# Another order of the units of one pair of heads, and the last product's polynomial regrouped in place in PSUM

## The chip, the cores and the metric

The kernel runs on one core of one Trainium2 chip. The metric is the device time of one execution in microseconds (us). It is taken as the median of several runs, and one further run was recorded by the profiler. The engines are named as the profile names them: PE (TensorE; PEld is its weight load), DVE (VectorE), ACT (ScalarE), POOL (GpSimd) and SP (SyncE, which in this kernel issues every DMA; SPq is its queue).

## What is computed

The reference runs three parts, each on the output of the one before it.

```python
# 1. attention by hash buckets: q, k, v are (2, 8, 768, 64), proj is (64, 6)
mask = q_bucket[:, :, :, None] == k_bucket[:, :, None, :]     # 6 sign bits of q @ proj and k @ proj
scores = np.where(mask, scale * np.matmul(q, k.transpose(0, 1, 3, 2)), -1000000000.0)
attn = softmax(scores)                                        # along the last axis
attn_out = np.matmul(attn, v)                                 # -> x of shape (1536, 512)
# 2. soft mixture of 8 experts with 4 slots each
logits = x @ phi                                              # (1536, 32)
slot_input = softmax(logits, axis=0).T @ x
slot_out[e] = np.maximum(slot_input[e] @ w1[e], 0.0) @ w2[e]
x = softmax(logits, axis=1) @ slot_out
# 3. the last product
h = x @ w_in                                                  # w_in is (512, 2048)
g = h - np.tanh(h)
out = g @ w_out                                               # w_out is (2048, 512)
```

## The kernel before, in words

**Attention** works on eight pairs of heads. Everything that is done for a pair is cut into units, and the strings `START`, `STEP` and `LAST` (lines 64 to 71) write out by hand in which order the units are issued. `STEP` is gone through once for each of the pairs 0 to 6, `LAST` for pair 7 (loop at line 709). Every engine executes what it is given in program order, so the string is the order of each engine's queue, SP's too. The map `role` (line 660) says for which pair a unit works: while the scores of pair i are made, units such as `m`, `l0` to `l3`, `d` and `f2` prepare pair i + 1, `t0`, `t1`, `b`, `h0` to `h3` and `kc` prepare pair i + 2, `qk` loads pair i + 3, and `xr`, `xe` and others that begin with x, and `lg`, finish pair i - 1. The units that matter here:

- `s0`, `s1` (`s_unit`, lines 493 to 513): one tile of 128 x 768 scores of one head, four matmuls into a PSUM tile (L497, L499). ACT takes the exponential (L501), POOL adds it to a running sum (L506, L512).
- `m` (`m_unit`, L446 and L447): two matmuls into a PSUM tile and a row maximum on DVE. There are twelve in a pair.
- `a` (`av_unit`, L520 and L524): the product with v, eight matmuls into PSUM tiles of its own. It does nothing while its two exponentials have not been issued.
- `l0` to `l3` (`lo`, L429, L431, L433, L436): the low halves of k and q, one subtraction of 64 x 768 on DVE each, with both inputs in SBUF. `l2` (L433) reads the copy that `kc` makes, `l3` (L436) one that `d` makes.
- `kc` (`kh1_copy`, one DMA kh<-KA) and `d` (`dups`, two or four DMAs QB<-QA and KB<-KA): copies from SBUF to SBUF.
- `wl` and `wc` (`win_load`, `win_cvt`): one 512 KB load of a piece of w_in into one of two buffers, and its conversion: ACT L174 and three DVE instructions (L178, L187, L192) by way of a PSUM tile `cl`. A `wl` issues nothing while two pieces wait for conversion.
- `t0`, `t1` (transposes, L353), `b` (`bits`, L362, after which eight DMAs QA<-rt and KA<-rt write the rows that `m` and `s` of that pair need), `f2` (`m_fin`, five or six DMAs QA<-row and z<-zrow), `v` (one load), `v1` (`v_unit`, three additions on POOL, L474 to L476), `v2`, `h0` to `h3` (ACT L406), `xr`, `xe`, `x2`, `x3` (L535 to L584), `lg` (`logits`, L594), `qk` (`load_qk`, four DMAs tq and tk, L321), `lp` (one 1 MB piece of the experts' weights, from pair 5 on), and `e00` to `e03` (work of pair 5 alone).

All PSUM tiles of these units but those of `a` come from one pool of three buffers (`ps`, line 272). A unit's first matmul therefore waits until an earlier unit's reader has freed a buffer.

**The experts** (`moe`, with the order `MOE`) follow. They read 32 pieces of 1 MB, and eight more of w_out, each through a ring of SBUF slots that open as attention closes its pools.

**The last product** (`class Ffn`) goes in 32 steps n, 16 blocks of h for each of two halves of the tokens. A step's block of h is 128 x 768 in two PSUM tiles `ph` of 512 and 256 columns. `h_mm` (L1167) makes them, `h_sq` has ACT write z = h^2 and w = (z + Q_A)^2 to SBUF (L1174, L1175), and `h_g` has DVE make g = Q_C h z (w + Q_B), a polynomial that stands for h - tanh(h). `split_hi` (ACT, L1205) and `split_lo` (POOL, L1210) split g into two parts, and `mm` multiplies them by w_out: six times three matmuls of 512 columns in a step (L1229 to L1231). In the steps of the first half, DVE also converts one block of w_out in each step (`cv_a2`, `b1`, `b2`: L178, L187, L192, all from SBUF to SBUF), and ACT and POOL split it (L1123, L1124). The first blocks are issued by the orders `MOE` and `RUN`, the rest by the loop at line 1254.

Of the kernel before, what the change touches and what calls it, by code (L numbers as in the profile page):

```python
# [15 lines left out]
ALU = mybir.AluOpType  # L16
# [33 lines left out]
Q_C = 17.0 / 315.0  # L50
Q_A = -(2.0 / 15.0) / (2.0 * Q_C)
Q_B = (1.0 / 3.0) / Q_C - Q_A * Q_A
# [12 lines left out]
        "h3.0 wq1p.0 m.0 m.0 m.0 l0.0 m.0 const.2 m.0 v.0 wk1a.0 m.0 m.0 m.0 wq0p.0 m.0 kc.0 m.0 "  # L65
        "m.0 qk.1 l2.0 m.0 wl.0 d.0 wc.0 wk0s.0 t0.1 f2.0 h1.1 t1.1 l1.0 h3.1 l3.0 v1.0 h2.1 "
        "kc.1 oi.1 b.1 v2.0 wc.0 wc.0 h0.1 qk.2 oi.2 wl.0").split()
STEP = ("s0 l1 d s1 a lp m xe s0 m xr e00 v m s1 m s0 l0 m lp m a m s1 l2 v1 m a m m m l3 a wl lp "
        "wc t1 s0 t0 s1 s0 m e01 h0 lp a lp h1 x2 lp wl f2 e02 s1 h3 lp v2 b e03 x3 wc wl s0 s1 "
        "h2 kc a lp wl wc lg qk").split()  # L70
LAST = ("s0 lp lp a s0 xe lp s1 s0 xr lp a s1 x2 x3 lg a lp s1 s0 s0 s0 lp s1 a s1 a s1 lp a lp").split()


# [52 lines left out]
def body(ctx: ExitStack, tc: tile.TileContext, q, k, v, proj, phi, w1, w2, w_in, w_out, cst, out, dbg=None):  # L126
    nc = tc.nc
# [7 lines left out]
    lg = const.tile([P, B * KT, NS], F32, name="lg")  # L135
# [114 lines left out]
    def attention():  # L250
# [458 lines left out]
        for i in range(NPR):  # L709
            for u in STEP if i < NPR - 1 else LAST:  # L710
                n = i + role.get(u, role.get(u[0], 0))
# [414 lines left out]
    class Ffn:  # L1126
# [49 lines left out]

        def h_g(self, n, p):
            z, w, g = self.views(n, p)
            nc.vector.scalar_tensor_tensor(w, w, Q_B, z, ALU.add, ALU.mult)  # L1179
            nc.vector.scalar_tensor_tensor(g, w, Q_C, self.ph[p], ALU.mult, ALU.mult)  # L1180


        def h_any(self, n):
# [155 lines left out]
```

## Time and profile before

| what | us |
|---|---|
| median of 3 runs | 519.05 (517.33 to 519.7) |
| the profiled execution, its own time | 519.88 |
| span of the profiled execution, first to last instruction | 518.0 |
| busy in that span: PE / PEld | 474.7 / 302.3 |
| busy in that span: DVE / ACT / POOL | 352.2 / 272.1 / 294.3 |

The time of the profiled execution is 1.9 us longer than its span: what lies around the program's first and last instruction. Its own time is 0.83 us above the median of the runs. All starts in the rows are us from the start of the span. A busy PE isn't PE at its peak, since matmuls are pipelined and a matmul's row includes its latency. PEclk is the share of TensorE's full clock that was granted.

### The profile page before, as it was taken

Reading aid. Unit: us, or ns where it says so; the run is one execution under the profiler, and the core shown is the slowest. Engines: PE = TensorE matmul, PEld = TensorE weight load, DVE = VectorE, ACT = ScalarE, POOL = GpSimd, SP = SyncE. Lnnn points to the kernel's source line nnn. Section 1 sums busy time; section 2 is a strip of 40 time slices with the busy share of each in tenths; the row PEclk is TensorE's granted clock in tenths of the full one; section 3 lists DMA queues with packets and bytes.
Section 4 is the critical chain, followed back from the end, with each engine's and each line's share of the span. In section 5 each row is a group of like instructions: output and inputs, shape, how many; then the busy total and the mean of one; then the engine's idle time right before and its main releaser. Section 6 shows DMA issues by size and latency. Waiting matters only on the chain.

```text
span 518.0 us, 7441 instructions
## 1 busy us (share of the span) xinstructions
PE 474.7 (92%) x2634; PEld 302.3 (58%) x2634; DVE 352.2 (68%) x493; ACT 272.1 (53%) x463; POOL 294.3 (57%) x243
## 2 busy tenths in 40 slices
PE   8798888998989989999999899889888888999996
PEld 3444555555545556565565634447666666888884
DVE  4949478696696776837622664569999998655552
ACT  6253654736537446364334111167777766767662
POOL 3867766777677677786874120025665664544442
PEclk9659899999999999999999999998999999999999
DMA  6518146091451712937679699994000000200003
GB/s 206 121 29 233 42 105 199 13 249 42 119 142 49 195 62 51 329 134 226 213 266 376 253 369 388 356 407 192 1 1 0 2 0 34 88 1 1 1 1 127
DMA packets 51572, 72.83 MB, mean 141 GB/s; under 512 B 25604, under 2 KB 33480, under 8 KB 51528
## 3 DMA queue, kind: packets, MB, share of 16 engines
q1 hardware_dynamic: 51528, 72.28, 42.9%
q8 instruction: 23, 0.38, 0.3%
q14 instruction: 21, 0.17, 0.1%
HBM read 60.08 MB, written 3.15 MB: 122 GB/s over the span
## 4 chain that ended last, share of the span: by engine, by line
PE 58%; DVE 32%; DMA 3%; SPq 3%; issue 2%; ACT 1%; DVEq 0%; ACTq 0%
PE pav L524 9%; DVE mx L447 9%; PE pst L497 6%; PE po L1229 5%; PE po L1230 5%; PE po L1231 5%; PE pst L499 5%; DVE win L1179 4%; PE pm L446 4%; DVE win L192 3%; DVE KB L429 3%; DVE win L1180 3%; DVE win L178 2%; DMA w<-in_moe_w_dram 2%; PE pl L594 2%
## 5 line engine op out<-in xcount | busy, mean ns | idle before, releaser
L512 POOL TENSOR_TENSOR es<-es,e 128x768 f32<-128x768 f32 x59 | 115.9, 1976 | 32.6 <-ACT e L501 32.2
L501 ACT ACTIVATE e<-pst 128x768 f32<-128x768 f32 x96 | 76.1, 809 | 87.7 <-PE pst L499 83.6
L447 DVE TENSOR_REDUCE mx<-pm 128x1 f32<-128x768 f32 x96 | 87.6, 953 | 36.8 <-PE pm L446 35.0
L524 PE MATMUL pav<-e,tv 128*64 128x256 f32 (+1 forms) x384 | 74.5, 506 | 0.0
L1210 POOL TENSOR_TENSOR split<-win,split 128x512 fp32r<-128x512 f32 x31 | 39.9, 1286 | 53.9 <-ACT split L1205 53.6
L1179 DVE SCALAR_TENSOR_TENSOR win<-win 128x512 f32<-128x512 f32 x64 | 51.0, 797 | 26.9 <-ACT win L1175 26.9
L497 PE MATMUL pst<-QA,KA 128*128 128x512 f32 x192 | 56.7, 377 | 10.8 <-DVE win L192 4.5
L446 PE MATMUL pm<-KA,QA 96*128 96x512 f32 x192 | 53.1, 380 | 2.6 <-DVE mx L447 1.1
L1210 POOL TENSOR_TENSOR ghl<-win,ghl 128x256 fp32r<-128x256 f32 x32 | 27.5, 859 | 47.5 <-ACT ghl L1205 45.1
L1229 PE MATMUL po<-w,split 128*128 128x512 f32 x128 | 51.3, 401 | 0.0
L1230 PE MATMUL po<-w,split 128*128 128x512 f32 x128 | 51.1, 399 | 0.0
L1231 PE MATMUL po<-w,split 128*128 128x512 f32 x128 | 50.8, 397 | 0.0
L499 PE MATMUL pst<-QB,KB 128*128 128x512 f32 x192 | 50.4, 344 | 0.0
L524 PEld LDWEIGHTS pav<-e,tv 128*64 128x64 f32 x384 | 24.3, 138 | 40.2 <-issue 39.3
L506 POOL TENSOR_TENSOR es<-e 128x768 f32<-128x768 f32 x16 | 29.2, 1828 | 28.7 <-PE pr L535 22.3
L497 PEld LDWEIGHTS pst<-QA,KA 128*128 128x128 f32 x192 | 30.2, 196 | 25.8 <-DVE mx L447 6.4
L446 PEld LDWEIGHTS pm<-KA,QA 96*128 96x128 f32 x192 | 30.2, 196 | 23.7 <-issue 6.8
L1175 ACT ACTIVATE win<-win,ct 128x512 f32<-128x512 f32 (+1 forms) x64 | 39.5, 617 | 2.1
L1180 DVE SCALAR_TENSOR_TENSOR win<-win,ph 128x512 f32<-128x512 f32 x64 | 35.5, 554 | 6.2
L1174 ACT ACTIVATE win<-ph 128x512 f32<-128x512 f32 (+1 forms) x64 | 30.7, 479 | 15.5 <-PE ph L1167 15.5
L499 PEld LDWEIGHTS pst<-QB,KB 128*128 128x128 f32 x192 | 30.1, 193 | 4.4
L1167 PE MATMUL ph<-hold,hold 128*128 128x512 f32 x64 | 21.9, 383 | 10.9 <-DVE win L1180 10.5
(243 smaller groups left out, 828.3 us busy)
## 6 DMA issues: line engine op xcount, KB each, us to landing
w<-in_moe_w_dram SPq DMA_DIRECT2D x32, 1024.0 KB
raw<-in_moe_w_in_dram SPq DMA_DIRECT2D x16, 512.0 KB
w<-in_moe_w_out_dram SPq DMA_DIRECT2D x8, 1024.0 KB
tv<-in_v_dram SPq DMA_DIRECT2D x8, 384.0 KB
out_dram<-win SPq DMA_DIRECT2D x12, 256.0 KB
tq<-in_q_dram SPq DMA_DIRECT2D x14, 192.0 KB
tk<-in_k_dram SPq DMA_DIRECT2D x14, 192.0 KB
QB<-QA SPq DMA_DIRECT2D x10, 192.0 KB
```

The lines of the kernel that those rows point to most:

```text
L446: nc.tensor.matmul(pm[:, c0:c1], QA[s][h][:96, c * P:(c + 1) * P], KA[s][h][:96, c0:c1], start=True, stop=True)
L447: nc.vector.reduce_max(mx[i][:, h * KT + c:h * KT + c + 1], pm, axis=AX.X)
L497: nc.tensor.matmul(pst[:, c0:c1], KA[s][h][:, c * P:(c + 1) * P], QA[s][h][:, c0:c1], start=True, stop=False)
L499: nc.tensor.matmul(pst[:, c0:c1], KB[t][h][:, c * P:(c + 1) * P], QB[t][h][:, c0:c1], start=False, stop=True)
L501: nc.scalar.activation(e, pst, AF.Exp, scale=0.125)
L512: eng.tensor_tensor(es[i, h][0], es[i, h][0], e, ALU.add)
L524: nc.tensor.matmul(pav[i][j][64 * h:64 * h + 64, :], tv[i][:, h, c, :], e2[h][:, c0:c1], start=False, stop=c == KT - 1, tile_position=(0, ...
L1179: nc.vector.scalar_tensor_tensor(w, w, Q_B, z, ALU.add, ALU.mult)
L1210: (eng or nc.gpsimd).tensor_tensor(gl[p], g, gh[p].bitcast(F32), ALU.subtract)
L1229: nc.tensor.matmul(po, gh[p][:, us], wo.half(f, 0), start=f == 0, stop=False)
L1230: nc.tensor.matmul(po, gh[p][:, us], wo.half(f, 1), start=False, stop=False)
L1231: nc.tensor.matmul(po, gl[p][:, us], wo.half(f, 0), start=False, stop=f == NF - 1)
```

## The change

The string `STEP` holds the same 72 units in another order, one line shorter in the file. In `h_g` the two DVE instructions for one tile are regrouped. Before, the first one made w = (w + Q_B) z in SBUF and the second one g = w Q_C h. Now the first makes h = z Q_C h in place in the PSUM tile of h, and the second g = (w + Q_B) h.

```diff
-STEP = ("s0 l1 d s1 a lp m xe s0 m xr e00 v m s1 m s0 l0 m lp m a m s1 l2 v1 m a m m m l3 a wl lp "
-        "wc t1 s0 t0 s1 s0 m e01 h0 lp a lp h1 x2 lp wl f2 e02 s1 h3 lp v2 b e03 x3 wc wl s0 s1 "
-        "h2 kc a lp wl wc lg qk").split()
+STEP = ("s0 a s1 l1 m s0 m xr xe m s1 wl v m m m s0 lp l0 m lp a m m s1 l2 e00 a m m d a wc wl e01 v1 s0 s1 t1 h0 lp l3 "
+        "wl s0 t0 m lp h3 a e02 lp v2 lp f2 h1 x2 s1 e03 b x3 wl wc s0 a h2 s1 qk lp lg kc lp wc").split()
...
         def h_g(self, n, p):
             z, w, g = self.views(n, p)
-            nc.vector.scalar_tensor_tensor(w, w, Q_B, z, ALU.add, ALU.mult)
-            nc.vector.scalar_tensor_tensor(g, w, Q_C, self.ph[p], ALU.mult, ALU.mult)
+            nc.vector.scalar_tensor_tensor(self.ph[p], z, Q_C, self.ph[p], ALU.mult, ALU.mult)
+            nc.vector.scalar_tensor_tensor(g, w, Q_B, self.ph[p], ALU.add, ALU.mult)
```

## Rows read from the trace of the kernel before

**Rows 1.** Windows: stretch, length, busy us of each engine, PEclk, DMA share, GB/s.

```profile
75.00:275.00 200.00, 189.80 (x1116) 113.33 (x1115) 136.99 (x182) 102.10 (x148) 146.57 (x104) 1.00 0.52 156
104.00:115.00 11.00, 10.77 (x58) 5.94 (x57) 10.16 (x10) 4.33 (x6) 7.56 (x4) 1.00 1.01 276
361.00:433.00 72.00, 62.03 (x253) 45.20 (x251) 67.81 (x88) 50.65 (x98) 44.77 (x37) 1.00 0.00 1
435.00:507.00 72.00, 72.00 (x320) 58.43 (x319) 41.97 (x67) 48.66 (x98) 31.92 (x32) 1.00 0.06 23
```

**Rows 2.** Chain of waits that ended last: start us, us, what; two neighbouring pairs.

```profile
104.87 0.85 PE pr L535 x8
...
138.54 0.85 PE pr L535 x8
```

**Rows 3.** Timeline of PE, one pair: start, us, what, idle before and releaser.

```profile
103.10 0.62 PE L446 MATMUL pm<-KA,QA 96*128 96x512 f32 x2
...
121.15 0.62 PE L497 MATMUL pst<-QA,KA 128*128 128x512 f32 x2 [1.16 <-DVE win L192]
...
128.89 0.63 PE L497 MATMUL pst<-QA,KA 128*128 128x512 f32 x2 [0.21 <-DVE xtok L584]
...
134.44 0.62 PE L497 MATMUL pst<-QA,KA 128*128 128x512 f32 x2 [0.90 <-ACT e L501]
```

**Rows 4.** Timeline of DVE in the same pair: the subtractions and a conversion.

```profile
108.34 2.26 DVE L429 TENSOR_TENSOR KB<-xk,KA 64x768 fp32r<-64x768 f32 x1
...
113.35 0.95 DVE L433 TENSOR_TENSOR KB<-xk,kh 64x768 fp32r<-64x768 f32 x1
...
117.80 1.05 DVE L436 TENSOR_TENSOR QB<-xq,QB 64x768 fp32r<-64x768 f32 x1
118.88 0.70 DVE L178 TENSOR_SCALAR cl<-raw 128x512 uint32<-128x512 uint32 x1
```

**Rows 5.** Timeline of POOL in the same pair.

```profile
107.95 1.83 POOL L506 TENSOR_TENSOR es<-e 128x768 f32<-128x768 f32 x1 [0.24 <-ACT e L501]
```

**Rows 6.** Timeline of SP's queue around the start of the same pair.

```profile
98.73 0.71 SPq L151 DMA_DIRECT2D QA<-rt  x1
...
103.14 0.53 SPq L151 DMA_DIRECT2D kh<-KA  x1
...
105.30 2.12 SPq L321 DMA_DIRECT2D tk<-in_k_dram  x2
```

**Rows 7.** Chain of waits, one DMA of rows from its issue to its landing.

```profile
66.78 2.66 DMA QA<-rt
```

**Rows 8.** Chain of waits in the last product: first and last of the seven alike.

```profile
362.98 0.95 DVE win L1179
...
432.92 0.93 DVE win L1179
```

**Rows 9.** Groups of DVE by shape, 362.9 to 432.9: busy us, mean ns, idle before.

```profile
L178 DVE TENSOR_SCALAR win<-w 128x512 uint32<-128x512 uint32 x12 | 13.6, 1130 | 0.0
...
L1179 DVE SCALAR_TENSOR_TENSOR win<-win 128x256 f32<-128x256 f32 x13 | 11.5, 885 | 0.0
L1179 DVE SCALAR_TENSOR_TENSOR win<-win 128x512 f32<-128x512 f32 x12 | 11.5, 955 | 0.0
L1180 DVE SCALAR_TENSOR_TENSOR win<-win,ph 128x512 f32<-128x512 f32 x13 | 8.9, 688 | 1.3
L187 DVE SCALAR_TENSOR_TENSOR win<-win 128x512 uint32<-128x512 uint32 x12 | 8.3, 692 | 1.2
L1180 DVE SCALAR_TENSOR_TENSOR win<-win,ph 128x256 f32<-128x256 f32 x12 | 5.1, 421 | 1.3
```

**Rows 10.** Groups over the whole span: a two-input instruction in place in PSUM.

```profile
L187 DVE SCALAR_TENSOR_TENSOR cl<-cg,cl 128x512 uint32<-128x512 uint32 x16 | 11.1, 696 | 6.2 <-ACT cg L174 5.2
```

**Rows 11.** Timeline of PE: the h matmuls of two neighbouring late steps.

```profile
456.93 0.52 PE L1167 MATMUL ph<-hold,hold 128*128 128x512 f32 x2
...
461.47 0.51 PE L1167 MATMUL ph<-hold,hold 128*128 128x512 f32 x2
```

## The prediction, made before the changed kernel ran

> **What bounds the kernel now.** I first read the busy time by stretches [rows 1], then the chain of waits in the two stages that the change touches, and last the timelines of the engines there. The stages have different bounds.
>
> In attention PE is busy for 189.8 of 200 us, DVE for 137 and POOL for 147 [rows 1]. Two neighbouring pairs stand 138.54 - 104.87 = 33.67 us apart [rows 2]. In such a pair PE idles at three places: 1.16 us until the last DVE instruction of a conversion (L192) has freed its PSUM buffer, 0.21 us until xtok has, and 0.90 us until an exponential has [rows 3], 2.27 us in all. So no order can take a pair below 33.67 - 2.27 = 31.4 us. Pairs 1 to 4 have conversions of w_in and repeat this pattern. From 204 on, in pairs 5 and 6, the timeline of PE shows no such idle row.
>
> In the first half of the last product the chain runs on DVE. DVE is busy for 67.81 of 72 us between 361 and 433, PE for 62.03 [rows 1]. The first and the last of seven equal entries of the chain, two steps apart each, are 432.92 - 362.98 = 69.94 us apart [rows 8]: twelve steps of 5.83 us. In the second half PE has no gap at all, 72.00 of 72 us [rows 1], and a step takes 461.47 - 456.93 = 4.54 us [rows 11]. There DVE is idle for two fifths of the time, so a cheaper DVE instruction is worth nothing. 4.54 us is also the floor that PE sets for the first half.
>
> **The polynomial.** The same number of DVE instructions stays. The first of each two, L1179, has both inputs in SBUF and takes 955 ns on 512 columns and 885 ns on 256 [rows 9]. That a half as wide takes as long says that most of it is waiting. L1180, with one input in PSUM, takes 688 and 421 ns [rows 9]. Subtraction on DVE shows the same wait in attention: L429 starts at 108.34, while POOL is in an addition until 107.95 + 1.83 = 109.78, and ends at 110.60, some 0.82 us after POOL is done; alike instructions that meet no POOL work take 0.95 us [rows 4, 5]. So a DVE instruction with two SBUF inputs waits out the POOL instruction that it meets. After the change both instructions have one input in PSUM. What the first one newly does is to write PSUM in place. The nearest row is the conversion in attention, one input in SBUF, one in PSUM and the output over it: 696 ns for 512 columns [rows 10]. I take L1180's durations for both. A step then saves (955 - 688) + (885 - 421) = 731 ns of DVE, and twelve steps 12 x 0.73 = 8.8 us, from 5.83 to 5.10 us a step.
>
> The bounds are 0, if the wait is only moved, and 12 x (5.83 - 4.54) = 15.5 us, if the conversions' waits shrink too and PE becomes the bound. There is room for that: L178 reads a single tile and takes 1130 ns where L187 takes 692 on the same size [rows 9], so it waits as well. Also the first instruction now needs z alone, so DVE can start while ACT still makes w. In the DVE-bound steps that costs and gives nothing, because ACT has finished w by then. The tile `ph` is freed, as before, after the second instruction. I leave the few blocks before 362 at no gain, since DVE shares that stretch with other small work.
>
> [...]
>
> **The order.** The same 72 units are issued, so no engine gets more work; what counts is who stands behind whom.
> - *Scores, `a` and `lg` at the seam of two pairs.* Before, `s0 l1 d s1` puts two score tiles behind one another, and the second waits 0.90 us for the exponential of the first. Now each `s0` there is followed by an `a`, eight matmuls in PSUM tiles of its own, before the next `s1`, and `wc` stands before `a` rather than before `s0 s1`. I expect the 0.90 and the 0.21 us to go: 1.1 us a pair.
> - *`l3` and `d`.* Before, `l3` (1.05 us, rows 4) stands on DVE ahead of the conversion that PE then waits for. Now it comes behind it, and two score tiles stand between conversion and transposes. That takes up to 1.05 us off the wait of 1.16 us. `d`'s four copies are issued later, behind `v`; `l3`, their reader, is later too.
> - *`m`.* Four to six maxima now precede `l0`. Whether `l0` and `l2` meet a POOL addition is open: a meeting costs 2.26 - 0.95 = 1.31 us [rows 4] on a DVE that in this stretch is as late as PE. Now `l0` does and `l2` doesn't; afterwards it can be both or none, so -1.3 to +1.3 us a pair, of which I take 0.5 as lost on the average.
> - *SP.* `kc` comes behind `qk`'s four loads, and `wl` and `v` ahead of `d`. No DMA is added. `v`'s load waits for `a` to free v's buffer, with `d` behind it. The rows for the first `m` (L446): in this pair the fourth of its DMAs is issued at 98.73 [rows 6], a landing takes 2.66 us [rows 7], so it is there at 101.4, 1.7 us before the `m` at 103.10 [rows 3]. When the 1.1 us at the seam go, 0.6 are left. I take 0.3 us a pair as lost.
> - *`v1`, `f2` after `v2`, `xr` before `xe`, `h0` to `h3`, `e00` to `e03`, `lp`, `wl`:* POOL's three additions of `v1`, ACT's copies and the loads move by a unit or two. POOL and ACT have idle time in every pair (147 and 102 busy of 200 us, rows 1), which hides them; without it they would add their own length, about 2 us for `v1`.
>
> Sum of a pair: -1.1 - 1.0 + 0.5 + 0.3 = -1.3 us. Four pairs make -5.2 us. The bounds are -2.27 x 4 = -9 and about +5 us, a new wait of 1.3 us in each of four pairs. Pair 0 loses its first `a` (its exponentials aren't issued yet), so PE reaches its first `m` earlier and waits there for rows, but it meets a shorter wait at the conversion; I put it at zero, within the 2.3 us of idle time of a later pair either way. Pairs 5 and 6 had nothing to lose: zero. The experts' weights come after these pairs in SP's queue, so the stage behind starts earlier by what attention saves.
>
> **Sum.** 519.88 - 8.8 - 5.2 = 505.9 us against the profiled execution's own time. That execution is 0.83 us above the median of the runs, so against the median it is 505.
>
> **The rivals.**
> 1. *Attention gains nothing*: a new wait of 1.3 us takes the place of the old ones. For it: three PSUM buffers, and DVE as late as PE. Then 519.05 - 8.8 = 510.3. Chance 0.12.
> 2. *PE becomes the bound of the first half*: all DVE waits shrink below 4.54 us a step. Against it: POOL still has 44.77 us of work in those 72 [rows 1], and L178 and L192 still meet it. Then 519.05 - 15.5 - 5.2 = 498.3. Chance 0.11.
> 3. *The waits move to the conversions*: L178, L187 and L192 meet what L1179 met, and a step stays at 5.83 us. Then 513.9. Chance 0.06. [...]
> 4. *Neither part does what it says*: 519. Chance 0.04.
> 5. *Slower: `l2` waits for its copy.* `kc` is issued when `qk`'s loads have been, 105.30 + 2.12 - 103.67 = 3.75 us later [rows 6], into a stretch in which the DMA engines are full (share 1.01 from 104 to 115, rows 1). `l2` now starts 10.2 us after `kc` was issued [rows 4, 6]. If the copy lands only as the burst ends, about 3 us too late, every maximum behind `l2` on DVE, and the matmuls that need their buffers, are late by that. It decides from (8.8 + 2.6 + 5.2) / 6 = 2.8 us in each of six pairs; at 3.5 us it gives 519.05 - 14 + 21 = 526. Against it: the copy lies behind four loads of 128 x 6 x 64 floats, 0.79 MB, and at 276 GB/s [rows 1] these take 2.8 us. Chance 0.05.
>
> **How the numbers follow.** The forecast, both parts paying about as worked out (498 to 511), has the remaining 0.62; its time is the prediction. A measurement of this kernel can tell about 0.5% from no change, 2.6 us. Faster than 516.4 us hold the forecast and rivals 1 to 3, 0.91, of which I take off 0.05 for ends that add up badly: 0.86. Within 0.5%: 0.08. Slower: 0.06. The range goes from 497, just under rival 2, to 514, rival 3, and leaves out some 2 in 10.
>
> **What the profile of the changed kernel would show.** The first instruction of `h_g` at 690 and 420 ns, without a spread, and POOL's halves of 256 columns shorter as well; double steps in the first half of 10.2 us instead of 11.67; no change in the second half; pairs 1 to 4 some 32.4 us apart, with no PE wait for an exponential at the seam; the first `m` close to its rows. The prediction is wrong if a double step stays above 11 us, if L178 and L192 grow by what the polynomial loses, if pairs are still 33 us apart or more, or if L433 or the first `m` waits for a DMA.

## The result, and the profile after

The kernel after took 499.69 us (median of 4 runs, 497.41 to 504.07), the kernel before 518.25 us beside it: ratio 0.965, 95% interval 0.9577 to 0.9722. A second set of runs gave 496.77 us against 519.43, ratio 0.9567 (0.9501 to 0.9634). The forecast was 505.0 us, range 497 to 514: the first set lies inside the range, the second just below it. The forecast had the direction and the size of the polynomial, and too little for the order.

In the kernel after every line number past 70 is one lower than before, since `STEP` takes one line less; in e5, e6 and e8 it is two lower.

The profiled execution of after has a span of 495.5 us, 22.5 less than before. I divide both spans at the same four events.

| stretch | before, us | after, us | difference |
|---|---|---|---|
| start to the first `pr` (start-up and pair 0) | 71.30 | 66.48 | -4.8 |
| first to last `pr` (the pairs 1 to 7) | 210.99 | 201.10 | -9.9 |
| last `pr` to the last product's first matmul (L1229, after L1228) | 68.4 | 69.0 | +0.6 |
| that matmul to the end | 167.3 | 158.9 | -8.4 |

The chain of waits of after shows both parts. Columns as in [rows 2]: start us, us, what.

```profile
66.48 0.85 PE pr L534 x8
98.43 0.85 PE pr L534 x8
128.96 0.85 PE pr L534 x8
159.52 0.84 PE pr L534 x8
190.06 0.78 PE pr L534 x8
...
359.20 0.69 DVE win L1179
364.29 0.70 DVE win L1179
...
410.08 0.69 DVE win L1179
```

Pairs stand 31.95, 30.53, 30.56 and 30.54 us apart, where before it was 33.67 [rows 2]. In the last product an entry of L1179 now comes once a step (before, once in two): (410.08 - 359.20) / 10 = 5.09 us a step, against 5.83 [rows 8].

The timeline of PE of after, around the same pair and in the second half of the last product:

```profile
98.43 0.85 PE L534 MATMUL pr<-es,ones 128*32 128x384 f32 x8 [1.19 <-DVE mx L446]
...
443.25 0.51 PE L1166 MATMUL ph<-hold,hold 128*128 128x512 f32 x2
447.79 0.51 PE L1166 MATMUL ph<-hold,hold 128*128 128x512 f32 x2
```

From there to the next `pr` at 128.95 one row of PE has an idle entry, 0.20 us ahead of the transposes at 112.57. The three waits of [rows 3], 2.27 us, are gone. The 1.19 us ahead of 98.43 belong to the interval of 31.95 us and don't come back in the next ones. The steps of the second half still take 4.54 us [rows 11].

The timeline of DVE of after in that pair, with what answers to [rows 4] (L428, L432 and L435 are the L429, L433 and L436 of before), and then two steps of the last product:

```profile
103.64 0.95 DVE L428 TENSOR_TENSOR KB<-xk,KA 64x768 fp32r<-64x768 f32 x1
...
107.84 0.96 DVE L432 TENSOR_TENSOR KB<-xk,kh 64x768 fp32r<-64x768 f32 x1
...
110.87 0.69 DVE L177 TENSOR_SCALAR cl<-raw 128x512 uint32<-128x512 uint32 x1
...
113.12 2.12 DVE L435 TENSOR_TENSOR QB<-xq,QB 64x768 fp32r<-64x768 f32 x1
...
370.88 0.42 DVE L177 TENSOR_SCALAR win<-w 128x512 uint32<-128x512 uint32 x1
371.40 1.59 DVE L186 SCALAR_TENSOR_TENSOR win<-win 128x512 uint32<-128x512 uint32 x1
...
373.64 0.69 DVE L1178 SCALAR_TENSOR_TENSOR ph<-win,ph 128x512 f32<-128x512 f32 x1
...
375.07 0.42 DVE L1178 SCALAR_TENSOR_TENSOR ph<-win,ph 128x256 f32<-128x256 f32 x1
```

POOL's timeline of after beside these:

```profile
103.88 2.40 POOL L511 TENSOR_TENSOR es<-es,e 128x768 f32<-128x768 f32 x1 [0.53 <-ACT e L500]
107.98 2.50 POOL L511 TENSOR_TENSOR es<-es,e 128x768 f32<-128x768 f32 x1 [1.70 <-ACT e L500]
...
112.59 6.11 POOL L511 TENSOR_TENSOR es<-es,e 128x768 f32<-128x768 f32 x3
...
370.87 1.58 POOL L1209 TENSOR_TENSOR split<-win,split 128x512 fp32r<-128x512 f32 x1 [0.18 <-ACT split L1204]
373.31 1.01 POOL L1209 TENSOR_TENSOR ghl<-win,ghl 128x256 fp32r<-128x256 f32 x1 [0.86 <-ACT ghl L1204]
```

And one row of POOL's timeline of before, beside `l2` (L433) of [rows 4]:

```profile
113.60 2.39 POOL L512 TENSOR_TENSOR es<-es,e 128x768 f32<-128x768 f32 x1 [1.32 <-ACT e L501]
```

`l0` takes 0.95 us instead of 2.26. It still meets an addition, but it starts first, at 103.64, 0.24 us ahead of POOL's, and now the addition is the one that waits: it takes 2.40 us, where the one that started ahead of `l0` before took 1.83 [rows 5]. `l2` (L432) does the same at 107.84, 0.14 us ahead of an addition that then takes 2.50 us. It did so before, too: at 113.35 it was 0.25 us ahead of POOL's 2.39 us. In all these rows the instruction that starts second pays, on whichever engine it runs. In after that is `l3` (L435), behind the conversion: it starts 0.53 us into an addition and takes 2.12 us.

In the last product the polynomial runs at 690 and 420 ns, though POOL is at work. The wait that is left sits on L186, the conversion's second instruction, with both inputs in SBUF: it starts 0.53 us into POOL's split, ends 0.54 us after it, and takes 1.59 us. The groups of DVE by shape in after, 345 to 415, columns as in [rows 9]:

```profile
L186 DVE SCALAR_TENSOR_TENSOR win<-win 128x512 uint32<-128x512 uint32 x13 | 19.9, 1529 | 1.2
L1178 DVE SCALAR_TENSOR_TENSOR ph<-win,ph 128x512 f32<-128x512 f32 x14 | 9.7, 689 | 0.4 <-ACT win L1173 0.4
...
L191 DVE SCALAR_TENSOR_TENSOR win<-w,win 128x512 uint32<-128x512 uint32 x13 | 9.5, 734 | 0.4
L1178 DVE SCALAR_TENSOR_TENSOR ph<-win,ph 128x256 f32<-128x256 f32 x14 | 5.9, 422 | 0.0
...
L177 DVE TENSOR_SCALAR win<-w 128x512 uint32<-128x512 uint32 x12 | 5.1, 422 | 0.0
```

Against [rows 9] the polynomial's first instruction fell from 955 to 689 and from 885 to 422 ns, L177 (before L178) from 1130 to 422, and L186 (before L187) rose from 692 to 1529. The conversion's three instructions together take 2685 ns. Before, with the 972 ns that L192 has in the same list of groups, it was 2794: its waits moved among the three and did not grow.

### The profile page after: what moved, and what is told of

It reads as the page before. It is cut to its first block, busy times and chain, and to the rows that moved or that the text cites. A ratio compares the mean times of both kernels' runs of the same rounds, so it can differ in the third digit from the quotient of the medians.

```text
span 495.5 us, 7422 instructions
## 1 busy us (share of the span) xinstructions
PE 467.0 (94%) x2634; PEld 302.5 (61%) x2634; DVE 332.7 (67%) x493; ACT 271.7 (55%) x463; POOL 298.6 (60%) x243
## 3 DMA queue, kind: packets, MB, share of 16 engines
HBM read 60.08 MB, written 3.15 MB: 128 GB/s over the span
## 4 chain that ended last, share of the span: by engine, by line
PE 60%; DVE 17%; DMA 7%; ACT 6%; SPq 4%; POOL 2%; issue 2%; DVEq 0%; ACTq 0%; POOLq 0%
PE pav L523 9%; PE po L1228 6%; PE po L1229 6%; PE po L1230 6%; PE pst L496 5%; PE pm L445 5%; PE pst L498 4%; DVE win L186 4%; DMA QB<-QA 3%; DVE mx L446 2%; SPq L150 2%; DVE win L1179 2%; PE pt L352 2%; PE po L913 2%; DVE win L191 2%
## 5 line engine op out<-in xcount | busy, mean ns | idle before, releaser
L511 POOL TENSOR_TENSOR es<-es,e 128x768 f32<-128x768 f32 x59 | 118.6, 2022 | 23.5 <-ACT e L500 22.8
L523 PE MATMUL pav<-e,tv 128*64 128x256 f32 (+1 forms) x384 | 72.9, 498 | 0.0
L1209 POOL TENSOR_TENSOR split<-win,split 128x512 fp32r<-128x512 f32 x31 | 44.0, 1420 | 45.6 <-ACT split L1204 45.5
L445 PE MATMUL pm<-KA,QA 96*128 96x512 f32 x192 | 55.6, 391 | 5.2 <-DMA QA<-rt 3.1
L1178 DVE SCALAR_TENSOR_TENSOR ph<-win,ph 128x512 f32<-128x512 f32 x64 | 35.7, 558 | 29.8 <-ACT win L1173 29.8
L1228 PE MATMUL po<-w,split 128*128 128x512 f32 x128 | 51.5, 402 | 0.0
L1229 PE MATMUL po<-w,split 128*128 128x512 f32 x128 | 51.4, 401 | 0.0
L1179 DVE SCALAR_TENSOR_TENSOR win<-win,ph 128x512 f32<-128x512 f32 x64 | 35.5, 555 | 8.6 <-ACT win L1173 0.5
L1230 PEld LDWEIGHTS po<-w,split 128*128 128x128 f32 x128 | 24.6, 192 | 5.7
```

The lines of the kernel that those rows point to most:

```text
L445: nc.tensor.matmul(pm[:, c0:c1], QA[s][h][:96, c * P:(c + 1) * P], KA[s][h][:96, c0:c1], start=True, stop=True)
L511: eng.tensor_tensor(es[i, h][0], es[i, h][0], e, ALU.add)
L523: nc.tensor.matmul(pav[i][j][64 * h:64 * h + 64, :], tv[i][:, h, c, :], e2[h][:, c0:c1], start=False, stop=c == KT - 1, tile_position=(0, ...
L1179: nc.vector.scalar_tensor_tensor(g, w, Q_B, self.ph[p], ALU.add, ALU.mult)
L1209: (eng or nc.gpsimd).tensor_tensor(gl[p], g, gh[p].bitcast(F32), ALU.subtract)
L1228: nc.tensor.matmul(po, gh[p][:, us], wo.half(f, 0), start=f == 0, stop=False)
```

## The experiments

### e1 and e2: each part alone

e1 is the kernel after with the old polynomial, e2 the kernel before with the new one.

```diff
 # e1: STEP as after, and in h_g
-            nc.vector.scalar_tensor_tensor(self.ph[p], z, Q_C, self.ph[p], ALU.mult, ALU.mult)
-            nc.vector.scalar_tensor_tensor(g, w, Q_B, self.ph[p], ALU.add, ALU.mult)
+            nc.vector.scalar_tensor_tensor(w, w, Q_B, z, ALU.add, ALU.mult)
+            nc.vector.scalar_tensor_tensor(g, w, Q_C, self.ph[p], ALU.mult, ALU.mult)
```

> The new order with the old polynomial. Theory (the two parts add up): the last product keeps its double steps of 11.67 us and gives nothing; attention's pairs stand 30.5 us apart as in the changed kernel, and the time is some 10 to 11 us below the kernel before, about 508 us. Rival (the order's gain hangs on the polynomial, or the stage of the experts' weights takes part of it back): less than 5 us below, above 513 us.

> The old order with the new polynomial. Theory (the two parts add up): attention unchanged with pairs 33.67 us apart, double steps of 10.18 us in the first half of the last product, 8 to 9 us below the kernel before, about 509.5 us. Rival (an earlier end of attention is what brings the double steps down): double steps above 11 us, less than 3 us below, above 515 us.

The kernel before took 517.99 us beside them. e1: 505.25 us, 0.9752 (0.9718 to 0.9787), 12.7 us less. Its pairs stand 30.5 us apart, and its steps take 5.84 us. e2: 509.0 us, 0.9811 (0.9775 to 0.9848), 9.0 us less; pairs 33.7 us, steps 5.09 us. Each part works in its own stage and leaves the other stage as it was. The gains add up to 21.7 us, between the 18.6 and the 22.7 us that the two sets of runs of after give. So the polynomial brought what was forecast, and the order over twice as much.

### e3 and e4: why the polynomial is cheaper

The regrouping has two effects: no instruction has both inputs in SBUF, and the first one needs only z. e3 keeps the first effect and drops the second. e4 has one instruction with an input in PSUM, as before, and its second one with both inputs in SBUF.

```diff
 # e3
-            nc.vector.scalar_tensor_tensor(self.ph[p], z, Q_C, self.ph[p], ALU.mult, ALU.mult)
-            nc.vector.scalar_tensor_tensor(g, w, Q_B, self.ph[p], ALU.add, ALU.mult)
+            nc.vector.scalar_tensor_tensor(self.ph[p], w, Q_B, self.ph[p], ALU.add, ALU.mult)
+            nc.vector.scalar_tensor_tensor(g, z, Q_C, self.ph[p], ALU.mult, ALU.mult)
 # e4
+            nc.vector.scalar_tensor_tensor(w, w, Q_B, self.ph[p], ALU.add, ALU.mult)
+            nc.vector.scalar_tensor_tensor(g, w, Q_C, z, ALU.mult, ALU.mult)
```

> The changed kernel with the in-place product started from w: h = (w + Q_B) h, then g = z Q_C h, so both instructions have one input in PSUM, but the first again needs ACT's second square. Theory (the inputs' place is what counts): double steps stay at 10.18 us and the time at that of the changed kernel within 1 us. Rival (starting DVE on z alone, before w is there, is part of the gain): DVE waits for w in every step, double steps above 10.6 us, 2 us or more slower than the changed kernel.

> The changed kernel with w = (w + Q_B) h first (one input in PSUM, output in SBUF) and g = w Q_C z second, both inputs in SBUF. Theory (a DVE instruction with two SBUF inputs waits out the POOL instruction that it meets): the second instruction takes over the long rows, above 750 ns on 512 or above 600 ns on 256 columns on the average, double steps go back to 11 to 12 us, 5 to 10 us slower than the changed kernel, about 505 to 509 us. Rival (the wait was for something else, such as w): both rows at 690 and 420 ns and the time of the changed kernel.

e3: 494.53 us, 0.955 (0.9501 to 0.9599), steps of 5.03 us, so the early start on z is worth nothing. The time is 5 us below the first set of after, where the theory allowed 1 us; e11 and e12 come back to that. e4: 508.97 us, 0.9824 (0.978 to 0.9868), steps of 6.21 us, longer than the 5.83 us of before. Groups of DVE by shape of e4, 345 to 415:

```profile
L177 DVE TENSOR_SCALAR win<-w 128x512 uint32<-128x512 uint32 x11 | 16.7, 1519 | 0.0
L191 DVE SCALAR_TENSOR_TENSOR win<-w,win 128x512 uint32<-128x512 uint32 x12 | 13.4, 1120 | 0.4
L1179 DVE SCALAR_TENSOR_TENSOR win<-win 128x256 f32<-128x256 f32 x12 | 12.0, 1002 | 1.2
...
L1179 DVE SCALAR_TENSOR_TENSOR win<-win 128x512 f32<-128x512 f32 x11 | 7.6, 693 | 1.1
L1178 DVE SCALAR_TENSOR_TENSOR win<-win,ph 128x512 f32<-128x512 f32 x11 | 7.4, 674 | 0.0
```

The instruction with two SBUF inputs on 256 columns takes 1002 ns and the one on 512 columns 693, so its length says where it meets POOL, not how much it computes. In the step around 373 the one on 512 columns starts at 373.09, 0.04 us ahead of POOL's L1123, which then takes 1.80 us where it takes 1.31 in after; the one on 256 columns starts at 374.22, in the middle of that L1123. The one with an input in PSUM takes 674, and the conversion's L177 and L191 wait again. That is the cause the prediction gave, with one thing added: in these rows what counts is which engine started first. On 256 columns the polynomial's first instruction, with one input in PSUM, takes 422 ns in after, and the one with two SBUF inputs 1002 here. L177, with a single input in SBUF, waits here all the same (1519 ns, in after 422); no row shows why.

### e5, e6, e8: the order's pieces put into the kernel before

e5 moves `l3` behind `t0`, e6 puts an `a` between the score tiles at the seam, e8 issues `l0` two maxima later.

```diff
 # e5
-... m a m m m l3 a wl lp wc t1 s0 t0 s1 s0 m e01 ...
+... m a m m m a wl lp wc t1 s0 t0 l3 s1 s0 m e01 ...
 # e6
-s0 l1 d s1 a lp m xe ... x3 wc wl s0 s1 h2 kc a lp wl wc lg qk
+s0 a l1 d s1 lp m xe ... x3 wc wl s0 a s1 h2 kc lp wl wc lg qk
 # e8
-... m s1 m s0 l0 m lp m a m s1 l2 ...
+... m s1 m s0 m lp m l0 a m s1 l2 ...
```

> The kernel before, whole, with one unit moved: l3 stands behind t0 instead of ahead of the conversion. Theory A (DVE's lateness at the conversion costs PE its wait of 1.16 us, and l3's 1.05 us are most of that lateness): the wait of a score tile for L192 falls to about 0.1 us, the pairs 1 to 4 come 32.6 us apart instead of 33.7, and the time is 4 to 5 us lower, some 513.5. Rival B (the wait is only moved: DVE is as late at the next place): the pairs stay within 0.3 us of 33.7, and the time within 1.5 us of the kernel before.

> The kernel before, whole, with two units moved at the seam of two pairs: an a stands between the last s0 and s1 of a pair and between the first s0 and the units behind it, so that a score tile no longer stands right behind the one whose buffer it needs. Theory A (the waits of 0.90 and 0.21 us at the seam are lost time): both go, pairs 1 to 4 come 32.6 us apart, and the time is 4 to 5 us lower, some 513.5. Rival B (DVE sets the pace in attention, and PE's wait at the seam is only where it shows): the wait at the conversion grows by what the seam loses, pairs stay within 0.3 us of 33.7, time within 1.5 us of before.

> The kernel before, whole, with l0 issued two row maxima later. Theory A (the subtraction of l0 meets POOL's addition and waits it out, and DVE sets the pace there): L429 falls from 2.26 to 0.95 us, pairs 1 to 4 come 32.4 us apart, 1.3 us less, and the time is 5 us lower, some 513. Rival B (DVE has slack there, or the maxima meet POOL in its place): L429 falls but pairs stay within 0.3 us of 33.7. Rival C: L429 meets the next POOL instruction and stays above 2 us.

The kernel before took 519.65 us beside these three and e7.

**e6** gained: 514.76 us, 0.9923 (0.9889 to 0.9957). Both waits at the seam are gone, and the wait at the conversion stays at 1.23 us. The pairs stand 32.31 and 32.52 us apart where before had 33.57 and 33.67: 1.2 us each, as theory A has it. The third took 34.64 us: there PE waited 1.71 us for L190 and the granted clock was 0.90 and 0.76 in the ten us around it. So the four pairs together gave 2.1 us. The larger part of the gain lies ahead of them and is not theory A's: the first `pr` comes at 67.44 instead of 71.30.

**e5** gained nothing and lost a little: 521.99 us, 1.0049 (1.0019 to 1.0079). The wait at the conversion fell to 0.20 us, as in theory A, but neither theory has what came next. The timeline of DVE of e5 has:

```profile
118.11 2.33 DVE L434 TENSOR_TENSOR QB<-xq,QB 64x768 fp32r<-64x768 f32 x1
```

The timeline of ACT of e5:

```profile
120.54 0.81 ACT L352 ACTIVATE xq<-pt 128x768 f32<-128x768 f32 x1 [2.82 <-DVE QB L434]
```

The timeline of PE of e5:

```profile
121.40 0.61 PE L444 MATMUL pm<-KA,QA 96*128 96x512 f32 x2 [1.60 <-ACT xq L352]
```

In its new place `l3` (L434) meets an addition on POOL (117.80 to 119.64) and ends 0.80 us after it. ACT, which is to write the next xq into a buffer that `l3` still reads, waits for it, and PE waits for the PSUM tile that ACT empties. Pairs are 34.8 and 34.9 us apart. In after `l3` meets POOL as well, but nobody stands behind it: it ends at 113.12 + 2.12 = 115.24, and ACT, which has a copy of `h0` and an exponential to do first, comes to xq at 115.77 without a wait.

**e8** lost: 530.45 us, 1.0206 (1.0151 to 1.026), pairs of 37.32, 36.37, 35.61 and 33.97 us. Rival C and more came true. The timeline of DVE of e8 in the pair after 107.49:

```profile
113.15 1.84 DVE L427 TENSOR_TENSOR KB<-xk,KA 64x768 fp32r<-64x768 f32 x1
...
116.01 2.45 DVE L431 TENSOR_TENSOR KB<-xk,kh 64x768 fp32r<-64x768 f32 x1
```

The timeline of PE of e8 there:

```profile
119.50 1.01 PE L444 MATMUL pm<-KA,QA 96*128 96x512 f32 x2 [1.98 <-DVE mx L445]
120.44 2.83 PE L522 MATMUL pav<-e,tv 128*64 128x512 f32 x8
```

Windows of e8, columns as in [rows 1]:

```profile
116.00:120.00 4.00, 2.02 (x11) 1.25 (x8) 3.96 (x3) 0.32 (x1) 3.10 (x4) 0.90 0.59 221
120.00:124.00 4.00, 4.00 (x14) 1.57 (x14) 3.87 (x6) 0.00 (x0) 0.45 (x1) 0.50 0.00 0
```

`l0` (L427) comes second to the next addition, and now `l2` (L431) to another, which started at 115.82: 1.84 + 2.45 = 4.29 us for the two, before 2.26 + 0.95 = 3.21 [rows 4]. PE, with three PSUM buffers, stands 1.98 us for the maximum behind them. In the windows PE is busy for half of the four us to 120, and then the granted clock is 0.50 for four us: the eight matmuls of `a` take 2.83 us in place of 1.51. So two maxima of delay, a change of nothing but places, cost 10.8 us.

### e7: a score tile and `l0` earlier, in the kernel after

```diff
-... xe m s1 wl v m m m s0 lp l0 m lp a m m s1 l2 ...
+... xe m s1 wl v m s0 lp l0 m m m lp a m m s1 l2 ...
```

> The kernel after, whole, with l0 issued two row maxima earlier, right behind the score tile whose sum POOL makes. Theory A (that l0 no longer meets POOL is worth 1.31 us a pair): L428 rises from 0.95 to about 2.2 us, pairs 1 to 3 go from 30.5 to 31.8 us, and the time is 4 to 5 us higher, some 504. Rival B (in the new order DVE has slack): L428 rises and the pairs stay within 0.3 us of 30.5, time within 1.5 us of after. Rival C: L428 stays at 0.95 there, nothing changes.

The edit moves `s0` and `lp` along with `l0`: all three stand two maxima earlier, and `l0` keeps its place behind that `s0`.

501.52 us, 0.9684 (0.9634 to 0.9734). The intervals of the runs overlap with those of after, so here the trace has to speak: pairs are 31.45 and 31.47 us apart, 0.93 more than in after, and from the first to the last `pr` it is 271.63 - 67.00 = 204.63 us, 3.5 more. The timeline of DVE of e7:

```profile
102.45 2.26 DVE L428 TENSOR_TENSOR KB<-xk,KA 64x768 fp32r<-64x768 f32 x1
```

The timeline of POOL of e7:

```profile
102.06 1.83 POOL L505 TENSOR_TENSOR es<-e 128x768 f32<-128x768 f32 x1 [0.24 <-ACT e L500]
```

These are the two rows of before again [rows 4, 5]: `l0` starts 0.39 us into POOL's addition, takes 2.26 us and ends 0.82 us after it. The pairs do what theory A says, at 0.93 of its 1.31 us; how much of that is due to the place of `s0` is not shown.

### The last four: after again, and the wait that is left

e11 is the kernel after once more, e12 is e3 once more, both on the same chip as the other two. e10 and e9 are e3 with L177, or the whole conversion of a block whose ACT part was done a step earlier, put between the polynomial's two tiles.

```diff
 # e10 and e9, in h_next
-                for p in range(2):
-                    self.h_g(n, p)
+                self.h_g(n, 0)
+                if mid:
+                    mid()
+                self.h_g(n, 1)
 # e9, what mid does (e10: cv_a2 alone)
+                def convert(f=cf - 1):
+                    self.cv_a2(f)
+                    wo.b1(f)
+                    wo.b2(f)
```

> The kernel after, once more, beside the next three on the same chip. Both theories: within 0.5% of its first measure, some 499.7 us, steps of 5.09 us in the first half of the last product.

> The kernel after with the two factors taken in the other order, h = (w + Q_B) h in place first, then g = z Q_C h, once more, beside the kernel after on the same chip. Theory A (which factor comes first is worth nothing: its steps took 5.03 against 5.09 us, 0.7 us over twelve, and the rest of its lead was the stage ahead of the last product): within 1.5 us of the kernel after. Rival B (it is a real gain): 4 to 5 us below it again.

> The kernel with (w + Q_B) h first, and of each step's conversion of a block of w_out the first instruction, the shift L177, issued between the polynomial's two tiles instead of behind them. Theory A (L186, with two inputs in SBUF, now waits out POOL's split, and only DVE's place at that moment counts): L186 meets POOL's split at another time, its 1530 ns change by some 0.3 us, a step takes 4.8 to 5.1 us, the time falls by 0 to 3 us. Rival B (DVE's busy time is what counts): same instructions, same step, 5.03 us, no change.

> The kernel with (w + Q_B) h first, and the whole conversion (L177, L186, L191), of the block whose part on ACT was done a step earlier, issued between the polynomial's two tiles. Theory A (L186 waits because it comes just after g has set POOL to work; between the tiles POOL works on another part): if L186 then meets no split, it takes 690 ns, DVE loses its 0.85 us a step, PE's 4.54 us bounds the step, and the time is up to 12 x 0.49 = 6 us lower. Rival B (the conversion meets POOL's split wherever it stands, or sets back the second g and POOL with it): L186 and L191 together stay at 2.2 us or more, the step at 5.0 us or above, time the same or higher.

| | us | ratio to before (519.43) | step, us |
|---|---|---|---|
| e11 | 496.77 | 0.9567 (0.9501 to 0.9634) | 5.09 |
| e12 | 494.76 | 0.9537 (0.9489 to 0.9584) | 5.03 |
| e10 | 497.03 | 0.9597 (0.9522 to 0.9673) | 5.17 |
| e9 | 511.98 | 0.985 (0.9792 to 0.9908) | 6.65 |

e11 came out 0.6% below the first set of after, a little more than the 0.5% expected. e11 and e12 overlap. (w + Q_B) h first has steps shorter by 0.06 us both times, 0.7 us over twelve. The 2 us between the medians are not more than the runs vary by, and rival B, 4 to 5 us, is out. Whether e12 is really faster than after stays open.

**e10** changes who waits and makes the sum a little larger; its step of 5.17 us is above both ranges. Per step L177 rose from 422 to 1065 ns and L191 from 692 to 918, and L186 fell from 1599 to 1013: 2996 in all against 2713 in e12. Here too the one that starts second waits, as with `l0` and `l2`: in e10 L177 at 369.25 starts 0.12 us after POOL's L1123 and takes 1.47 us. In after L177 and POOL's split start within 0.01 us of each other, too close to tell by; there L177 keeps its 0.42 and the split takes 1.58 us, where e9's takes 1.31.

**e9** did away with the wait and lost 17.2 us against e12. The timeline of DVE of e9 in one step:

```profile
377.46 0.69 DVE L186 SCALAR_TENSOR_TENSOR win<-win 128x512 uint32<-128x512 uint32 x1
378.19 0.69 DVE L191 SCALAR_TENSOR_TENSOR win<-w,win 128x512 uint32<-128x512 uint32 x1
...
381.89 0.70 DVE L1178 SCALAR_TENSOR_TENSOR ph<-win,ph 128x512 f32<-128x512 f32 x1 [2.15 <-ACT win L1174]
```

The timeline of ACT of e9 in the same step:

```profile
378.92 0.63 ACT L1122 ACTIVATE w<-win 128x512 fp32r<-128x512 f32 x1 [2.58 <-DVE win L191]
...
380.01 0.62 ACT L1204 ACTIVATE split<-win 128x512 fp32r<-128x512 f32 x1
...
381.14 0.73 ACT L1174 ACTIVATE win<-win,ct 128x512 f32<-128x512 f32 x1
```

L186 takes 0.69 us. But ACT's queue has L1122, which copies the block that L191 has just finished, ahead of the split of g and of the next z and w. So ACT stands 2.58 us for L191, and DVE then stands 2.15 us for w. Waiting for one another, the two engines make a loop of 6.65 us. Theory A had its first half right (690 ns) and its conclusion wrong; rival B foresaw the time, by another way. 4.54 us a step was not reached.

## Why the prediction was right, and where not

**The polynomial: right, size and cause.** -8.8 us were forecast; e2 measured -9.0, and the profiled span lost 8.4 in that stage. Steps of 5.10 us were forecast and 5.09 measured. The two durations taken from L1180, 688 and 421 ns [rows 9], came out as 689 and 422. The bounds of 0 and 15.5 us stayed far off. An input in PSUM made the instruction no longer on 512 columns: 689 ns for the in-place product, 693 for the one with two SBUF inputs in e4. Wrong were two details: POOL's halves of 256 columns did not get shorter (988 ns in after between 345 and 415, before 966 in the stretch of [rows 9]), and the conversion's waits did change. They gathered on L186 without growing in sum, so rivals 2 and 3 both missed.

**The order: the right sign, a term of the sum mis-sized.** -1.3 us a pair in four pairs, -5.2 us, was forecast. The four intervals changed by -1.62, -3.15, -3.26 and -2.00 us. In the pair of the rows, by the prediction's own terms:
- Seam, -1.1: e6 alone gives -1.2. Right.
- Collision, +0.5: the step that failed first. It averaged over meetings as if they were chance, and it took 0.95 us to mean that an instruction meets no POOL work, where `l2` of [rows 4] met an addition and was first. The string fixes where each subtraction stands against POOL's additions, and with it which engine waits. In after `l0` and `l2` are first in every pair and POOL waits (from the first `pr` to 200 us they take 0.95 or 0.96 us each time, and the additions beside them 2.38 to 2.50); e7, which moves an `s0` as well, prices the place of `l0` at -0.93.
- The rows for the first `m`, +0.3: no row of PE in that pair waits for a DMA. Zero.
- Conversion, -1.0: what is left is -3.15 + 1.2 + 0.93 = -1.0, and the wait for the conversion is gone. But this was not shown by itself, and e5 shows that moving `l3` alone doesn't bring it: it depends on where POOL's addition and `t0` stand.

**"No order can take a pair below 31.4 us": wrong.** Pairs take 30.53 us. The floor took the idle time marked in PE's rows for all there was. Windows of the same pair, before and after, columns as in [rows 1], show what it missed:

```profile
104.87:138.54 33.67, 30.97 (x174) 18.12 (x175) 25.31 (x34) 18.24 (x27) 24.17 (x17) 1.00 0.42 116
98.43:128.95 30.52, 30.31 (x174) 18.16 (x175) 24.84 (x33) 17.86 (x26) 24.21 (x17) 1.00 0.49 124
```

Before, PE was idle for 33.67 - 30.97 = 2.70 us, not 2.27; the row of 0.20 us below is one that the prediction left out. And the same 174 matmuls keep PE busy for 0.66 us less in after, so rows of a busy PE hold short waits too. The timeline of PE of before has the same six transposes twice:

```profile
117.33 0.88 PE L353 MATMUL pt<-ct,tk 128*128 128x128 f32 x6
117.97 0.59 PE L497 MATMUL pst<-QA,KA 128*128 128x512 f32 x2
...
119.11 0.88 PE L353 MATMUL pt<-ct,tq 128*128 128x128 f32 x6 [0.20 <-ACT xk L354]
```

Ahead of 117.97 they keep PE for 0.64 us, while their row says 0.88. The score tile behind the second ones starts at 121.15 with 1.16 us marked as idle [rows 3], which leaves 0.88, a quarter of a us more. Which other rows make up the 0.66 us is not shown.

**Pair 0 at zero: wrong.** The first `pr` comes 4.8 us earlier. 1.3 of them lie ahead of `STEP` (the first transposes start at 20.66 instead of 21.99) and aren't the change's: that start lies between 20.29 and 22.57 in the traces of all kernels here, whatever the order. The rest, 3.5 us, is what the prediction set off against a wait for rows. It is no accident of one run: from the first transposes to the first `pr` it is 45.0 to 46.8 us in all nine traces with the new order or e7's, and 49.3 in those of before and e2. The wait for rows is there: PE stands 3.10 us for QA<-rt at 33.82. But it falls into a stretch where the granted clock is 0.50 anyway (after, 30 to 34 and 34 to 38). Before, PE stood later. The timeline of PE of before in pair 0:

```profile
54.24 1.54 PE L353 MATMUL pt<-ct,tq 128*128 128x128 f32 x6 [2.51 <-DVE win L192]
```

Windows of before, right behind:

```profile
53.00:56.00 3.00, 1.76 (x7) 1.68 (x8) 1.15 (x2) 0.18 (x1) 1.56 (x1) 0.65 0.26 85
56.00:59.00 3.00, 3.00 (x14) 2.05 (x14) 0.68 (x1) 2.47 (x4) 0.95 (x1) 0.79 0.23 90
```

Around and behind that wait the granted clock was 0.65 and 0.79; in after it is 1.00 in every window from 42 to 66. e6, which also takes the first `a` out of pair 0, shows the same: 3.11 us of wait at 34.15, first `pr` at 67.44. How the 3.5 us divide between the shorter wait and the clock is not shown.

**Right as forecast:** pairs 5 and 6 (-0.56 and +0.70 us), the second half of the last product (4.54 us), and the stage between (+0.6). **Rival 5**, `l2` waiting for the copy of `kc`, did not come: L432 follows a maximum with no idle time, at 107.84, 8.9 us after the copy was issued at 98.94. **Rival 1** is out by e1, **rival 4** by both. That the first set lies inside the range is in part luck: the range reached down to 497 for rival 2, which did not come, and what used that room is the larger gain of the order.

## What to carry to other kernels

Where a DVE instruction with both inputs in SBUF met POOL's work in the rows above, the one that started second waited: `l0` cost DVE 1.31 us where POOL was first and nothing where DVE was, and then POOL paid some 0.6 us (2.40 against 1.83). So price each meeting by who starts first and by who stands behind the one that waits, not by an average; with one operand in PSUM the polynomial's first instruction took 690 ns on 512 columns and 422 on 256 and showed no such wait (e2, e3). A wait that is moved is worth something only if nobody stands behind the new place: before moving a unit, follow its reader and the buffer that it frees through the next two engines (e5, e9). The idle time marked on a nearly full engine is not a bound for what another order can save: 2.27 us were marked in the pair of the rows, and it became 3.15 us shorter.

## What the runs showed that I had not expected

- Some waits of PE cost more than themselves: the granted clock was 0.50 behind the wait of 1.98 us in e8, where the eight matmuls of `a` took 2.83 us in place of 1.51, and 0.76 in the five us behind the one of 1.71 us in e6, while behind the 1.16 us of before it stayed at 1.00 [rows 1, 3].
- The same shift instruction on 512 columns takes 0.42 us from SBUF to SBUF and 0.69 us into a PSUM tile (L177 in after, at 370.88 and 110.87). The 1130 ns of before [rows 9] are 0.7 us above the first.
- A meeting in which DVE is first costs POOL: beside `l0` and `l2` its additions take 2.40 and 2.50 us instead of 1.83. Its split, which starts within 0.01 us of L177, takes 1.58 us in after and 1.31 in e9, where nothing on DVE gets in its way.
